# A GpSimd drain between two experts' scatters, and gate logits of the last 256 tokens made token by expert

## The chip, the core and the metric

The kernel runs on one core of a Trainium2 chip. The metric is the device time of one execution in microseconds (us). Three executions are shown for the kernel before, and one execution was profiled.

## What is computed

Three layers one after the other: causal attention with a decay, a dense gated layer, and a mixture of experts that sends each of the 2304 tokens to one of 8 experts. The part that the change touches is the third:

```python
def _moe2_ref(x, w_gate, w_output_gate, w1, w2):
    logits = x @ w_gate                      # (2304, 512) @ (512, 8)
    e_idx = np.argmax(logits, axis=1)
    ...
    gate_w = probs[np.arange(N), e_idx]
    eom = 1.0 / (1.0 + np.exp(-(x @ w_output_gate)))
    for e in range(E):
        mask = e_idx == e
        h = np.maximum(x[mask] @ w1[e], 0.0)
        ye = h @ w2[e]
        out[mask] = gate_w[mask, None] * eom[mask, e, None] * ye
```

## The kernel before

**Attention and the dense layer.** Attention works on 16 pairs of heads. The dense layer (class `MoE1`) runs six groups of 256 hidden columns over chunks of tokens; its result `y` lies in SBUF as feature by token. In the last group the chunks are four of 384 tokens and three of 256 (list `CL`, L912). As soon as a chunk of the last group is done, `Route.chunk` (L434) makes its routing.

**Routing of a chunk.** For each of four blocks of 128 features ScalarE rounds `y` to `yh` (L443), VectorE makes the rest `yl` (L444), and TensorE multiplies with the gate matrix `gw`, 16 columns (8 of the gate, 8 of the output gate) in two parts, as the stationary side and the tokens as the moving side (L445, L446). The product is expert by token. VectorE copies it to SBUF as `lt` (L448), and TensorE transposes it in tiles of 128 tokens to token by expert (L451). `rows` (L505) transposes `y` itself to token rows (L510), and ScalarE copies these out as `yr` (L513), which SyncE writes to the DRAM tensor `yd`. ScalarE copies the second part of the logits as `l0` (L456), VectorE adds the first as `lg` (L457), and then a chain of small VectorE operations follows: maximum (L462), candidates (L464, L465), the expert chosen (L468, L470), ranks of the tokens within their experts with matmuls by `ones` and `U` (L474 to L478), positions (L487 to L495), and for each tile of 128 tokens the matrices `val` and `sel` (L499, L502), whose product (L503) is added into the table `slots`. PSUM tiles of this class come from the pool `rt_ps`, which has two buffers. `finish` (L541) turns `slots` into the lists of token numbers `sl_idx` (L546).

**The experts.** Each expert has 304 slots in tiles of 128, 128 and 48 rows. `MoE2.pull` (L607) gathers its token rows from `yd` by an indirect DMA that GpSimd issues, `gates` (L634) gathers its gate values; both go through `gather` (L639), which keeps the last one in `self.pmark`. `g1` and `g2` are the two matmuls in four quarters. `put` (L685) transposes a tile of the result, scales it by the gates (L696, or L694 on VectorE) and calls `scatter` (L699), an indirect DMA of GpSimd to the rows of `out`. Expert e - 1's three `put` calls come between expert e's quarters (L969 and L970). Tokens beyond an expert's 304 slots go through blocks: one block is worked on between the experts (`block_a` from L973, with gathers of weights through L640, and `block_b` at L979), others in the loop of L985, which runs `trip` times; with these inputs it runs zero times. After the quarters the gates of expert 7 are gathered (L980), the last `g2` runs (L981), and the three last `put` calls follow (L982 and L983).

**What sets the order.** The tile framework traces the calls in this order, orders each engine's instructions and adds semaphores. `tc.issue_after(x)` puts the instructions of its block that run on the engine of `x` behind `x` in that engine's queue, without a wait for its completion. GpSimd's queue holds gathers, scatters, the read of the trip count (L984), the entry of the loop and the end of the program. The engine that is written `POOL` in the profile is GpSimd; a `q` behind an engine's name marks its sequencer.

Of the kernel before, what the change touches and what calls it, by code (L numbers as in the profile page):

```python
# [9 lines left out]
F32 = mybir.dt.float32  # L10
# [10 lines left out]
N = B * S  # L21
# [5 lines left out]
CW = 384  # L27
# [378 lines left out]
class Route:  # L406
# [27 lines left out]
    def chunk(self, t0, n, slots):  # L434
        nc, cst, rp, rp1 = self.nc, self.cst, self.rp, self.rp1
        nt = n // 128
        g0 = t0 // 128
        yc = self.y[:, :, t0:t0 + n]
        lp = self.ps.tile([128, 512], F32, name="rt_ps")
        for k in range(4):  # L440
            yh = rp.tile([128, CW], F32R, name="yh")
            yl = rp.tile([128, CW], F32R, name="yl")
            nc.scalar.activation(yh[:, :n], yc[:, k], ACTF.Copy)  # L443
            nc.vector.tensor_sub(yl[:, :n], yc[:, k], yh[:, :n].bitcast(F32))  # L444
            nc.tensor.matmul(lp[:32, :n], self.gw[:, k], yh[:, :n], start=k == 0, stop=False)  # L445
            nc.tensor.matmul(lp[:16, :n], self.gw[:, k, 0], yl[:, :n], start=False, stop=k == 3)  # L446
        lt = rp1.tile([32, CW], F32, name="lt")
        nc.vector.tensor_copy(lt[:, :n], lp[:32, :n])  # L448
        lp = self.ps.tile([128, 512], F32, name="rt_ps")
        for t in range(nt):  # L450
            nc.tensor.transpose(lp[:, 32 * t:32 * (t + 1)], lt[:, 128 * t:128 * (t + 1)], cst["ident"][:32, :32])  # L451
        self.rows(t0, nt)
        lg = self.lg[:, g0:g0 + nt]
        lv = lp[:, :32 * nt].rearrange("p (t c) -> p t c", t=nt)
        l0 = rp1.tile([128, nt, 16], F32, name="l0")
        nc.scalar.activation(l0, lv[:, :, 16:], ACTF.Copy)  # L456
        nc.vector.tensor_add(lg.rearrange("p t a e -> p t (a e)"), lv[:, :, :16], l0)  # L457
        ll = lg[:, :, 0]
        sm = lambda nm, k=1: rp1.tile([128, nt] if k == 1 else [128, nt, k], F32, name=nm)
        bc = lambda a, k=E_: a.unsqueeze(2).to_broadcast([128, nt, k])  # L460
        mx = self.mx[:, g0:g0 + nt]
        nc.vector.tensor_reduce(out=mx, in_=ll, axis=AX.X, op=ALU.max)  # L462
        cand = sm("cand", E_)
        nc.vector.tensor_tensor(cand, ll, bc(mx), op=ALU.is_ge)  # L464
        nc.vector.scalar_tensor_tensor(cand, cand, -16.0, cst["eiota"].unsqueeze(1).to_broadcast([128, nt, E_]),  # L465
                                       op0=ALU.mult, op1=ALU.add)
        mn = sm("mn_")
        nc.vector.tensor_reduce(out=mn, in_=cand, axis=AX.X, op=ALU.min)  # L468
        oh = self.oh[:, g0:g0 + nt]
        nc.vector.tensor_tensor(oh, cand, bc(mn), op=ALU.is_equal)  # L470
        ohf = oh.bitcast(F32)
        rk = self.ps.tile([128, 512], F32, name="rt_ps")
        rv = rk[:, :nt * E_].rearrange("p (t e) -> p t e", e=E_)
        nc.tensor.matmul(rv, cst["ones"], self.acc.unsqueeze(1).to_broadcast([128, nt, E_]), start=True, stop=False)  # L474
        nc.tensor.matmul(rv, cst["U"], oh, start=False, stop=nt == 1)
        for t in range(nt - 1):
            m = nt - 1 - t
            nc.tensor.matmul(rv[:, t + 1:], cst["ones"], oh[:, t:t + 1].to_broadcast([128, m, E_]),  # L478
                             start=False, stop=m == 1)
        base = sm("base")  # L480
        nc.vector.tensor_scalar(base, mn, 16.0, float(PB * 128), op0=ALU.add, op1=ALU.mult)
        for t in range(nt):
            nc.vector.tensor_add(self.acc, self.acc.bitcast(F32), ohf[:, t])
        pf = sm("pf")
        rs = sm("rs_", E_)
        for t in range(nt):
            nc.vector.tensor_tensor_reduce(out=rs[:, t], in0=rv[:, t], in1=ohf[:, t], scale=1.0, scalar=base[:, t:t + 1],  # L487
                                           op0=ALU.mult, op1=ALU.add, accum_out=pf[:, t:t + 1])
        pi = rp1.tile([128, nt], I32, name="pi")
        nc.vector.tensor_copy(pi, pf)  # L490
        li = rp1.tile([128, 2, nt], I32, name="li")
        nc.vector.tensor_scalar(li[:, 0], pi, 127, 0, op0=ALU.bitwise_and, op1=ALU.logical_shift_right)
        nc.vector.tensor_scalar(li[:, 1], pi, 7, 0, op0=ALU.logical_shift_right, op1=ALU.logical_shift_right)
        lf = rp1.tile([128, 2, nt], F32, name="lf")
        nc.vector.tensor_copy(lf, li)  # L495
        for t in range(nt):
            g = g0 + t
            val = rp.tile([128, NBLK], F32R, name="val_")
            nc.vector.tensor_scalar(val, cst["iota"][:, :NBLK], lf[:, 1, t:t + 1], cst["tok1"][:, g:g + 1],  # L499
                                    op0=ALU.is_equal, op1=ALU.mult)  # L500
            sel = rp.tile([128, 128], F32R, name="sel_")
            nc.vector.tensor_scalar(sel, cst["iota"][:, :128], lf[:, 0, t:t + 1], None, op0=ALU.is_equal)  # L502
            nc.tensor.matmul(slots[:, :NBLK], sel, val, start=(g == 0), stop=(g == NT - 1))  # L503
# [87 lines left out]
class MoE2:  # L591
# [107 lines left out]
    def scatter(self, o, ix, free=True):  # L699
        ins = self.nc.gpsimd.indirect_dma_start(out=self.out, out_offset=bass.IndirectOffsetOnAxis(ap=ix, axis=0),  # L700
                                                in_=o, in_offset=None, bounds_check=N - 1, oob_is_err=False)
        if free:
            if self.nput:
                self.tc.declare_no_dep(ins.ins, group="rows", reason="each token row is scattered by one slot only")
            self.tc.add_to_no_dep_group("rows", ins.ins)
            self.nput += 1
# [161 lines left out]
def tile_kernel(tc, io, out, dbg=None):  # L868
    nc = tc.nc
    with ExitStack() as ctx:  # L870
# [65 lines left out]
        with ExitStack() as c2:  # L936
            wc = pool(c2, "wC", 12, reuse_waits="tile")
            wts.pools = [wab[0], wc, wc]
            m2 = MoE2(tc, c2, cst, io, wts, rt.yd, rt.gd, info, out)
            pblk = pool(c2, "blk")  # L940
            m2.braw = pool(c2, "blk_raw")
            cur = cp.tile([128, 1], F32, name="cur")
            nc.vector.memset(cur, 0.0)
            gwk = pool(c2, "gwk")
            m2.L[0, 0] = w00
            with tc.issue_after(rt.mark[0].ins), tc.issue_after(rt.mark[1].ins):
                m2.pull(0)
                m2.warm(WARM[0], info["id1"])
                for t in range(NSB):
                    m2.pre(0, t)  # L950
                    m2.warm(WARM[1 + t], m2.YG[0][min(t, 1)])
            with tc.issue_after(m2.mark[0].ins), tc.issue_after(m2.mark[1].ins):
                for u in range(1, 4):
                    m2.L[0, u] = load_expert(nc, io, wts, m2.raw, 0, u)
            st = [(e, u) for e in range(E_) for u in range(4)]
            for i, (e, u) in enumerate(st):
                if u == P0 and e + 1 < E_:
                    m2.pull(e + 1)
                if u == 0 and e:
                    m2.gates(e - 1)  # L960
                m2.g1(e, u)
                if i == GI:
                    rt.gate_rows(m2.ps_g, gwk)
                    rt.blocks(info, gwk)
                if u >= P1 and u < P1 + NSB and e + 1 < E_:
                    m2.pre(e + 1, u - P1)
                if i:
                    m2.g2(*st[i - 1])
                if u < NSB and e:  # L969
                    m2.put(e - 1, u)  # L970
                if (e, u) == (4, 3):
                    with tc.issue_after(m2.pmark.ins):
                        blk = m2.block_a(pblk, cur, rt)  # L973
                if e == 5:
                    with tc.issue_after(m2.pmark.ins):
                        blk[4](2)
                if (e, u) == (6, 2):
                    with tc.issue_after(m2.mark[0].ins), tc.issue_after(m2.mark[1].ins):
                        m2.block_b(pblk, cur, True, blk)  # L979
            m2.gates(E_ - 1)  # L980
            m2.g2(*st[-1])  # L981
            for t in range(NSB):  # L982
                m2.put(E_ - 1, t)  # L983
            trip = nc.values_load(info["trip"][0:1, 0:1], min_val=0, max_val=NOB + E_)  # L984
            with tc.For_i(0, trip, 1):  # L985
                m2.block(pblk, cur, rt, False)
# [35 lines left out]
```

## Time and profile before

| What | Time |
|---|---|
| Three runs | 1008.58, 1012.9, 1015.99 us |
| Median | 1012.9 us |
| Profiled execution, own time | 1005.57 us |
| Its span, first to last instruction | 1003.8 us |
| Granted TensorE clock over the span | 0.975 |

The span is what the rows below are taken from; 1.8 us of the profiled execution's time lie around it. The profiled execution was 7.3 us faster than the median of the three runs.

### The profile page before, as it was taken

To read this page: it belongs to the slowest core of one execution; us is meant where nothing else is said; L and a number is where in the kernel's file an instruction comes from. 1 tells how busy PE (TensorE), PEld (TensorE's weight loads), DVE (VectorE), ACT (ScalarE), POOL (GpSimd) and SP (SyncE) were. 2 spreads that over 40 slices of the span, in tenths; PEclk is the share of its full clock that TensorE was granted. 3 is DMA by queue.
4 is the path that set the end of the run, shared out by engine and by line. 5 is a ranking of instruction groups with operands and counts; after the bars stand their busy time and mean duration, and the time that the engine had idled before them with its cause. 6 is when DMAs were issued, how large, how long until landed. Compare 5 with 4: busy or idle time off the path is not lost.

```text
span 1003.8 us, 16493 instructions
## 1 busy us (share of the span) xinstructions
PE 944.4 (94%) x6282; PEld 847.5 (84%) x6282; DVE 597.3 (60%) x1421; ACT 411.9 (41%) x903; POOL 228.4 (23%) x205
## 2 busy tenths in 40 slices
PE   8899999999999999999999999999899999699893
PEld 5555555579999999999999999998799999699692
DVE  6566776759457468468467455677865554343720
ACT  5556666644343132132132123333554555244620
POOL 1244444442021011011011000000244434631111
PEclk9999999999999999999999999999899999989997
DMA  5344444313122012012012000113576576750400
GB/s 165 102 130 114 143 134 136 107 43 105 43 64 63 1 53 74 1 47 81 1 42 64 1 1 22 43 58 133 185 226 185 183 229 184 231 174 27 132 30 25
DMA packets 53088, 94.83 MB, mean 94 GB/s; under 512 B 5954, under 2 KB 27086, under 8 KB 53007
## 3 DMA queue, kind: packets, MB, share of 16 engines
q1 hardware_dynamic: 47503, 79.58, 26.0%
q0 software_dynamic: 5504, 14.17, 4.2%
q8 instruction: 50, 0.82, 0.3%
q14 instruction: 31, 0.25, 0.1%
HBM read 84.10 MB, written 10.16 MB: 94 GB/s over the span
## 4 chain that ended last, share of the span: by engine, by line
PE 57%; issue 16%; DVE 12%; POOL 6%; ACT 3%; DMA 3%; POOLq 0%; SPq 0%; DVEq 0%; ACTq 0%
PE ps_g L365 23%; PE ps_y L383 12%; PE ps_s L144 4%; DVE dt L316 3%; PE avy L201 3%; PE ps_t L185 3%; PE m_psg L659 3%; PE m_psy L674 2%; PE avx L201 2%; POOL out L700 2%; DVE dt L317 1%; ACT e L158 1%; POOL w L329 1%; DVE e L151 1%; DVE dt L315 1%
## 5 line engine op out<-in xcount | busy, mean ns | idle before, releaser
L365 PE MATMUL ps_g<-xth,w 128*128 128x384 f32 (+1 forms) x1184 | 308.6, 331 | 0.0
L365 PEld LDWEIGHTS ps_g<-xth,w 128*128 128x128 f32 x1184 | 213.1, 188 | 0.6
L365 PE MATMUL ps_g<-xtl,w 128*128 128x384 f32 (+1 forms) x592 | 196.1, 331 | 0.0
L383 PE MATMUL ps_y<-hh,w 128*128 128x384 f32 (+1 forms) x592 | 161.2, 333 | 2.9 <-DVE y L389 2.2
L659 PE MATMUL m_psg<-ygh,w 128*128 128x304 f32 x512 | 117.4, 311 | 1.2 <-ACT b_o L809 0.8
L674 PE MATMUL m_psy<-h2h,w 128*128 128x304 f32 x512 | 114.6, 306 | 0.5 <-issue 0.5
L383 PEld LDWEIGHTS ps_y<-hh,w 128*128 128x128 f32 x592 | 107.1, 188 | 5.8 <-DVE y L389 4.0
L329 POOL TENSOR_TENSOR w<-ds,w 128x512 fp32r<-128x512 f32 x36 | 49.8, 1384 | 271.9 <-ACT w L328 271.4
L365 PEld LDWEIGHTS ps_g<-xtl,w 128*128 128x128 f32 x592 | 111.2, 188 | 0.1
L158 ACT ACTIVATE e<-e,mx 128x320 f32<-128x320 f32 (+4 forms) x160 | 88.5, 555 | 51.7 <-DVE mx L151 51.2
L586 DVE TENSOR_TENSOR w<-raw,w 128x1024 fp32r<-128x1024 f32 x64 | 76.8, 1222 | 37.9 <-ACT w L585 22.4
L383 PE MATMUL ps_y<-hl,w 128*128 128x384 f32 (+1 forms) x296 | 97.9, 331 | 0.5 <-DVE hl L373 0.5
L372 ACT ACTIVATE hh<-hs 128x384 fp32r<-128x384 f32 (+1 forms) x74 | 38.2, 517 | 134.4 <-DVE hs L371 134.4
L370 DVE SCALAR_TENSOR_TENSOR hs<-hs,ps_g 128x384 f32<-128x384 f32 (+1 forms) x74 | 40.0, 541 | 86.4 <-ACT hs L369 86.4
L659 PEld LDWEIGHTS m_psg<-ygh,w 128*128 128x128 f32 x512 | 87.4, 193 | 1.8 <-ACT b_o L809 0.9
L674 PEld LDWEIGHTS m_psy<-h2h,w 128*128 128x128 f32 x512 | 85.5, 188 | 0.3
L151 DVE CUSTOM_DVE_ANT_0 e<-ps_s,mask 128x320 f32<-128x320 f32 (+4 forms) x160 | 62.6, 429 | 37.5 <-PE ps_s L144 36.6
L585 ACT ACTIVATE w<-raw 128x1024 fp32r<-128x1024 f32 x64 | 67.5, 1059 | 34.1 <-PE m_psg L659 13.3
L659 PE MATMUL m_psg<-ygl,w 128*128 128x304 f32 x256 | 78.4, 306 | 0.5 <-DVE ygl L627 0.5
L389 DVE TENSOR_TENSOR y<-ps_y,y 128x384 f32<-128x384 f32 (+1 forms) x124 | 67.2, 542 | 19.0 <-PE ps_y L383 18.2
L369 ACT ACTIVATE hs<-ps_g 128x384 f32<-128x384 f32 (+1 forms) x74 | 35.4, 479 | 104.6 <-PE ps_g L365 104.5
L674 PE MATMUL m_psy<-h2l,w 128*128 128x304 f32 x256 | 77.4, 302 | 0.0
(305 smaller groups left out, 1520.0 us busy)
## 6 DMA issues: line engine op xcount, KB each, us to landing
raw<-w SPq DMA_DIRECT2D x64, 512.0 KB
qk<-qk SPq DMA_DIRECT2D x16, 576.0 KB
v<-vL SPq DMA_DIRECT2D x16, 448.0 KB
raw<-mg SPq DMA_DIRECT2D x12, 512.0 KB
raw<-mv SPq DMA_DIRECT2D x12, 512.0 KB
raw<-mo SPq DMA_DIRECT2D x12, 512.0 KB
rb<-rd SPq DMA_DIRECT2D x16, 288.0 KB
yd<-yr SPq DMA_DIRECT2D x18, 256.0 KB
```

The source lines that it names most:

```text
L144: nc.tensor.matmul(ps[a][b:, :n], x, y, start=c == 0, stop=c == 1, tile_position=(h, b))
L151: nc.vector.tensor_tensor_reduce(out=o, in0=x, in1=y, scale=-0.125, scalar=BIGF if prev[a] is None else prev[a][b:], op0=ALU.add, op1=ALU. ...
L158: nc.scalar.activation(es[a][b:, :w], es[a][b:, :w], ACTF.Exp, bias=prev[a][b:], scale=-1.0, accum_out=rs[b:, c:c + 1])
L201: nc.tensor.matmul(self.X[x][64 * a:64 * a + 64, d0:d0 + n], v[k0:k0 + k, a, j], self.T[g, a][k0:k0 + k, o:o + n], start=g == 0, stop=g == ...
L329: nc.gpsimd.tensor_sub(lo, s3, hi.bitcast(F32))
L365: nc.tensor.matmul(ps[:, :n], w[:, k, fs], x[:, k], start=(k == 0 and c == 0), stop=(k == 3 and c == 2))
L383: nc.tensor.matmul(ps[:, :n], w[:, f, ds], h[:, f, :n], start=(f == 0 and c == 0), stop=(f == 1 and c == 2))
L389: nc.vector.tensor_add(y, ps[:, :n], y)
L585: nc.scalar.activation(hi, r, ACTF.Copy)
L586: nc.vector.tensor_sub(lo, r, hi.bitcast(F32))
L659: nc.tensor.matmul(ps[:, :C], w[:, k, fs], x[:, k], start=(k == 0 and c == 0), stop=(k == 3 and c == 2))
L674: nc.tensor.matmul(self.P[e][d][:, :C], w[:, f, ds], h[:, f], start=(u == 0 and f == 0 and c == 0), stop=(u == 3 and f == 1 and c == 2))
```

## The change

Two edits. In `Route.chunk`, for the chunk that ends at the last token (the last 256), the sides of the logit matmuls are exchanged: tiles of 128 tokens of `yh` and `yl` are the stationary side and `gw` the moving one, so that the product is token by expert at once, and the copy `lt` and its transposes are left out. In the main program a drain of GpSimd is issued behind the last gather and the last scatter traced so far, those of `gates(7)` and of expert 6's third tile, and the three scatters of expert 7 come behind it.

```diff
@@ Route.chunk
         g0 = t0 // 128
+        last = t0 + n == N
         yc = self.y[:, :, t0:t0 + n]
...
             nc.vector.tensor_sub(yl[:, :n], yc[:, k], yh[:, :n].bitcast(F32))
+            if last:
+                for t in range(nt):
+                    ts = slice(128 * t, 128 * (t + 1))
+                    nc.tensor.matmul(lp[:, 32 * t:32 * (t + 1)], yh[:, ts], self.gw[:, k], start=k + t == 0, stop=False)
+                    nc.tensor.matmul(lp[:, 32 * t:32 * t + 16], yl[:, ts], self.gw[:, k, 0], start=False,
+                                     stop=k == 3 and t == nt - 1)
+                continue
             nc.tensor.matmul(lp[:32, :n], self.gw[:, k], yh[:, :n], start=k == 0, stop=False)
             nc.tensor.matmul(lp[:16, :n], self.gw[:, k, 0], yl[:, :n], start=False, stop=k == 3)
-        lt = rp1.tile([32, CW], F32, name="lt")
-        nc.vector.tensor_copy(lt[:, :n], lp[:32, :n])
-        lp = self.ps.tile([128, 512], F32, name="rt_ps")
-        for t in range(nt):
-            nc.tensor.transpose(lp[:, 32 * t:32 * (t + 1)], lt[:, 128 * t:128 * (t + 1)], cst["ident"][:32, :32])
+        if not last:
+            lt = rp1.tile([32, CW], F32, name="lt")
+            nc.vector.tensor_copy(lt[:, :n], lp[:32, :n])
+            lp = self.ps.tile([128, 512], F32, name="rt_ps")
+            for t in range(nt):
+                nc.tensor.transpose(lp[:, 32 * t:32 * (t + 1)], lt[:, 128 * t:128 * (t + 1)], cst["ident"][:32, :32])
@@ MoE2.scatter
+        self.smark = ins
@@ tile_kernel
             m2.gates(E_ - 1)
+            with tc.issue_after(m2.pmark.ins), tc.issue_after(m2.smark.ins):
+                dr = nc.gpsimd.drain()
             m2.g2(*st[-1])
-            for t in range(NSB):
-                m2.put(E_ - 1, t)
+            with tc.issue_after(dr.ins):
+                for t in range(NSB):
+                    m2.put(E_ - 1, t)
```

## Rows read from the trace of the kernel before

**Rows 1.** The page, busy time by engine (us, share of the span, instructions)

```profile
PE 944.4 (94%) x6282; PEld 847.5 (84%) x6282; DVE 597.3 (60%) x1421; ACT 411.9 (41%) x903; POOL 228.4 (23%) x205
```

**Rows 2.** Stretches: length, busy PE PEld DVE ACT POOL, PEclk, DMA share, GB/s

```profile
992.00:994.00 2.00, 0.00 (x0) 0.00 (x0) 0.00 (x0) 0.00 (x0) 0.00 (x0) 0.50 0.00 0
...
995.60:1003.00 7.40, 0.00 (x0) 0.00 (x0) 0.00 (x0) 0.00 (x0) 0.00 (x0) 0.50 0.00 1
```

**Rows 3.** Line L1018, program's end: ns min/median/max, first and last start in us

```profile
L1018 POOLq DRAIN  x3: 46/108/7277, 995.7 to 1003.5; - x3
...
L1018 DVEq DRAIN  x2: 10/14/17, 995.3 to 1003.2; - x2
```

**Rows 4.** Line L985, loop entry, GpSimd's sequencer, the same view

```profile
L985 POOLq INC_SWDGE_SEM  x1: 1919/1919/1919, 992.0 to 992.0; - x1
```

**Rows 5.** Line L1015, program's start, GpSimd's sequencer, the same view

```profile
L1015 POOLq INC_SWDGE_SEM  x1: 27/27/27, 0.1 to 0.1; - x1
...
L1015 POOLq DRAIN  x1: 169/169/169, 0.3 to 0.3; - x1
```

**Rows 6.** Timeline, last chunk's logits: start us, us, engine, line, operation

```profile
699.37 0.28 PE L445 MATMUL rt_ps<-yh,gw 128*32 128x256 f32 x1
...
699.48 0.28 PE L446 MATMUL rt_ps<-yl,gw 128*16 128x256 f32 x1
...
700.74 0.29 PE L446 MATMUL rt_ps<-yl,gw 128*16 128x256 f32 x1
...
701.07 0.41 DVE L448 COPY lt<-rt_ps 32x256 f32<-32x256 f32 x1
701.41 0.34 DVE L499 TENSOR_SCALAR val__7402<-cst,lf 128x152 fp32r<-128x152 f32 x1
...
701.54 0.31 PE L451 MATMUL rt_ps<-cst,lt 32*128 32x32 f32 x2 [0.50 <-DVE lt L448]
...
701.77 0.42 PEld L510 LDWEIGHTS rt_ps<-cst,y 128*128 128x128 f32 x4
...
701.88 0.20 ACT L456 ACTIVATE l<-rt_ps 128x32 f32<-128x32 f32 x1 [1.73 <-PE rt_ps L451]
...
702.14 0.27 DVE L502 TENSOR_SCALAR sel__7409<-cst,lf 128x128 fp32r<-128x128 f32 x1
...
702.33 0.17 DVE L457 TENSOR_TENSOR lg_all<-rt_ps,l 128x32 f32<-128x32 f32 x1
...
707.83 1.28 POOL L640 DMA_INDIRECT yg<-yd,sl_idx  x1 [168.35 <-DVE sl_idx L546]
```

**Rows 7.** Line L640, all gathers that GpSimd issues, the view of rows 3

```profile
L640 POOL DMA_INDIRECT yg<-yd,sl_idx x24: 922/1026/1703, 707.8 to 904.3; - x24
L640 POOL DMA_INDIRECT gate<-gd,sl_idx x24: 931/1004/1521, 742.5 to 903.1; - x24
L640 POOL DMA_INDIRECT b_r<-w,b_wi x12: 997/1002/1212, 802.7 to 875.6; - x12
L640 POOL DMA_INDIRECT b_y<-yd,b_d x1: 1446/1446/1446, 833.2 to 833.2; - x1
L640 POOL DMA_INDIRECT b_g<-gd,b_d x1: 1005/1005/1005, 834.9 to 834.9; - x1
```

**Rows 8.** Line L700, all scatters that GpSimd issues, the view of rows 3

```profile
L700 POOL DMA_INDIRECT out<-o,sl_idx x24: 887/1246/1777, 755.0 to 989.4; - x24
L700 POOL DMA_INDIRECT out<-b_o,b_d x1: 1274/1274/1274, 951.5 to 951.5; - x1
```

**Rows 9.** Timeline of GpSimd, 970 to 991 us

```profile
975.94 0.90 POOL L700 DMA_INDIRECT out<-o,sl_idx  x1 [6.17 <-ACT o L696]
986.82 0.99 POOL L700 DMA_INDIRECT out<-o,sl_idx  x1 [9.99 <-ACT o L696]
988.12 0.98 POOL L700 DMA_INDIRECT out<-o,sl_idx  x1 [0.30 <-issue]
989.41 0.89 POOL L700 DMA_INDIRECT out<-o,sl_idx  x1 [0.30 <-issue]
```

## The prediction, made before the changed kernel was run

> **What bounds the kernel now.** I read the page first, then the end of the span by stretches, then the sequencer rows of the last source lines, then the queue of GpSimd, and last the timeline around the final routing chunk. The page says that TensorE is busy for 94% of the span [rows 1], so most edits elsewhere would be hidden under it. The stretches of the end show where that isn't so [rows 2]: from 992 us on no engine has anything busy, and from 995.6 to 1003 us, 7.4 us, even the DMA share is 0.00. The page's chain does not explain this, because it ends at the last scatter. The sequencer rows of the program's end (L1018) do [rows 3]: the DRAIN of VectorE takes 10 to 17 ns, but GpSimd executes three, of 46, 108 and 7277 ns, the long one first, at 995.7 us. 995.7 + 7.28 gives 1003.0, and the span ends at 1003.8: everybody waits for GpSimd's drain. Just ahead of it, in the barrier at the loop of L985, which runs zero times here, GpSimd spends 1919 ns on one INC_SWDGE_SEM at 992.0 [rows 4]. At the start of the program, with no transfer of GpSimd behind them, the same two operations cost 27 and 169 ns [rows 5]. So 9.2 us of the end are two sequencer instructions of GpSimd, with all data already landed.
>
> The second place that the change touches is the hand-over from the dense layer to the experts, at 699 to 708 us, where TensorE waits for a chain of small VectorE operations and GpSimd's first gather waits until 707.83 [rows 6].
>
> **Part one, the drain.** What does the long drain pay for? Since the start GpSimd has issued 24 + 24 + 12 + 1 + 1 gathers (L640) [rows 7] and 24 + 1 scatters (L700) [rows 8], 87 in all. The two drains behind the long one find no new transfer and cost 46 and 108 ns; so the long one clears something that stays cleared. If that is one record for each of GpSimd's transfers, one costs (7277 - 108) / 87 = 82 ns. The change drains after the 84th, so the last drain has three left: 108 + 3 x 82 = 355 ns. It gives back 7277 - 355 = 6.92 us on the bare end of the span. The bounds are 7277 - 46 = 7.23 us and, if the price is for a queue that was used at all, nothing.
>
> The early drain itself: it stands behind the scatter of expert 6's last rows, which starts at 975.94 and takes 0.90, so it begins at 976.84 at the latest. Behind it on GpSimd wait the three scatters of expert 7, the first at 986.82 when ScalarE has made its rows [rows 9], then GpSimd's read of the trip count and the loop's barrier. 84 records take 6.9 us, to 983.7. If it must first wait for the transfers in flight, I add at most 1.7 us (the last scatter's issue ends at 990.30, and the DMA share is gone by 992 [rows 2, 9]): 985.4. That is 1.4 us ahead of need, so I cost the early drain at nothing; its cover is expert 7's matmuls, which don't use GpSimd. Without that cover, each microsecond past 986.82 moves all three scatters, which follow each other without a gap, and so the end, by a microsecond. The bounds of its length are 46 ns and, since one and the same scatter takes from 887 to 1777 ns here [rows 8], twice 7.28, 14.6 us; I take 6.9, the row of the same operation scaled by its count.
>
> INC_SWDGE_SEM: the trace has it at 1919 ns with 87 transfers behind it and at 27 ns with none. Nothing shows how it depends on them; a gain is bounded by 0 and 1.89 us. I take 1.4, three quarters: the operation is the same, as it was for the drain, but at the program's start it may also have fewer semaphores to handle. With a short drain the next thing late is the last scatter's transfers, which I leave as they are.
>
> A rule that speaks against this part: the Trainium skill, "VectorE: DVE Perf Modes", section "The DRAIN you can't avoid", says that drains of the preamble and postamble are boilerplate of about 12 ns on all five engines. VectorE's drains here, 10 to 17 ns, agree; GpSimd's 7277 ns doesn't [rows 3]. By that rule the added drain would cost about 12 ns and clear nothing, the 7.28 us would belong to something else that the last row happens to cover, and the time would be that of the first rival below.
>
> **Part two, the logits of the last 256 tokens.** Removed: VectorE's copy of the logits (L448), which holds that engine from 701.07 until the next operation starts at 701.41, 0.34 us; two transposes on TensorE at 701.54; and the hand-overs around them. Before, the last logit matmul starts at 700.74, ScalarE's copy l0 at 701.88 and the sum lg at 702.33 [rows 6]. Added: 16 matmuls with a stationary side of 128 tokens in place of 8 with 256 moving tokens. A load of 128 x 128 takes 0.42 / 4 = 0.11 us from one to the next (L510), the old pairs 0.11 (699.37 to 699.48) [rows 6], and the two transposes took 0.31, so 16 x 0.11 - 8 x 0.11 - 0.31 = 0.6 us more of TensorE, most of it in its waits for yh and yl. Three of them follow the last yl: 700.74 + 3 x 0.11, plus the 0.34 that lay between the start of the transposes and l0 at 701.88, gives l0 at about 701.4, half a microsecond sooner. But VectorE is not free then: val and sel of the chunk before (701.41 to 702.14) stand ahead of lg, and they move up only by the 0.34 us of the copy. If lg is put ahead of them it gains up to 0.8, and they come back later in the same chain. I take 0.34 us, and bounds of -0.6 (all the added TensorE work bare) and +0.8. The chain behind lg ends in the gather at 707.83, so the 0.34 is passed on to the experts. The chunk takes one buffer of rt_ps less; the row transposes (L510) may start earlier for the first tile and wait for lg for the second, and neither has a follower before the ranks are needed. No DMA is added or moved past another queue.
>
> **Sum.** 6.92 + 1.4 + 0.34 = 8.7 us. The profiled execution took 1005.6 us with a span of 1003.8; it becomes 996.9. It lies 7.3 us under the median of the shown runs, 1012.9; the terms don't depend on what makes the runs differ, so I take the same 8.7 us from the median: 1004.2 us, 0.86% less.
>
> **The rivals.**
> First, the drain's price is fixed, or is not the drain's: every drain after use costs 7.28 us, or the added one costs next to nothing. For it: the trace has no drain after few transfers, so that the price grows with their count is not shown. Against it: the price was gone for the two drains behind the long one, as it would be if it were paid for records that are then cleared. Only part two is left: 1012.9 - 0.3 = 1012.6.
>
> Second, the early drain is slowed beside running work, by as much as scatters are (a factor 2 in [rows 8]): 14.6 us from 976.84 ends at 991.4, 4.6 us past need, while the last one is short all the same. 8.7 - 4.6 = 4.1: 1008.8. Against it: the stretch has a light VectorE and little DMA, and the scatters there take 0.90 to 0.99 [rows 9], the low end.
>
> Third, slower than before: the price is for a used queue and not for a count, and the early drain is slowed as well. The place is the queue of GpSimd ahead of 986.82; it decides as soon as the early drain takes more than 10.0 us (986.82 - 976.84), as nothing is given back at the end. At 14.6 us: +4.6 - 0.3, 1017.2. Against it: it needs both of the above at once.
>
> **How the numbers follow.** Forecast 0.80, first rival 0.13, second 0.05, third 0.02. The forecast's own range is 1003.3 to 1006.6 (INC_SWDGE_SEM from 0 to 1.89, part two from -0.6 to +0.8). The range given: down to the three upper bounds, 7.23 + 1.89 + 0.8 = 9.9, and the lowest shown run (4.3 under the median), 1012.9 - 9.9 - 4.3 = 998.7, rounded to 999; up to the second rival and the highest shown run (3.1 above the median), 1011.9, rounded to 1012. Left out are a good half of the first rival, the third, and the tails, some 0.17. A measurement of this kernel tells about 1%, 10.1 us, from no change. The forecast lies 1.4 us short of that, inside what runs scatter, so I give a third of it to faster: 0.27. Slower by over 1% would need the third rival with an early drain of over 20 us, or a bad draw of the first: 0.02. The rest is 0.71.
>
> **What would show it.** Right: a second long DRAIN of GpSimd, some 7 us, that starts near 977 us; the last first drain under 0.5 us; INC_SWDGE_SEM under 1 us; the first scatter of expert 7 still ready with its rows; the gather of expert 0 at about 707.5. Wrong: a last drain that still takes 7 us, an added drain of nanoseconds, or a scatter of expert 7 that starts right where the added drain ends.

## The result, and the profile after

The changed kernel takes 1000.42 us (median of 8 runs, 995.82 to 1003.49). The kernel before, run beside it, has a median of 1009.16 us over 8 runs, lower than the 1012.9 us of the three that were known. By these medians the gain is 8.74 us, 0.87%. The ratio on record, which is taken over the runs and isn't the quotient of the two medians, is 0.9902, with a 95% interval of 0.9874 to 0.9931: 0.98% faster. The interval lies clear of no change, the gain is just under the 1% that the prediction took as the least that a measurement tells, and by a 2% verdict it is "same". The profiled execution of the changed kernel took 1001.02 us, with a span of 999.2.

Here is the page of the changed kernel, busy time by engine, the line that answers to [rows 1]:

```profile
PE 944.8 (95%) x6288; PEld 848.4 (85%) x6288; DVE 598.5 (60%) x1420; ACT 411.2 (41%) x903; POOL 229.2 (23%) x205
```

Nothing in it tells of the gain. TensorE has 6 matmul instructions more: 16 in place of 8, without the two transposes. VectorE has one instruction less, the copy. No engine works less than before by more than a microsecond, because the time that went was never busy time on this page.

It is found where [rows 3 to 5] were found. These are GpSimd's sequencer rows of the changed kernel by source line (ns min/median/max, first and last start in us); the change moves the lines, so L1031 is the program's end, L998 the loop's entry, L992 the added drain and L1028 the program's start:

```profile
L1031 POOLq DRAIN  x3: 52/98/302, 998.1 to 999.0; - x3
...
L1031 DVEq DRAIN  x2: 10/14/17, 997.7 to 998.7; - x2
...
L998 POOLq INC_SWDGE_SEM  x1: 244/244/244, 996.1 to 996.1; - x1
...
L992 POOLq DRAIN  x1: 8069/8069/8069, 979.2 to 979.2; - x1
...
L1028 POOLq INC_SWDGE_SEM  x1: 27/27/27, 0.1 to 0.1; - x1
...
L1028 POOLq DRAIN  x1: 174/174/174, 0.3 to 0.3; - x1
```

The long drain of the end is gone: 7277 ns became 302. INC_SWDGE_SEM went from 1919 to 244. The long one now stands on L992. It starts at 979.24 us, while the scatter ahead of it is still to be issued, and its 8069 ns contain that wait; it ends at 987.31. GpSimd's own timeline of the changed kernel tells the rest (start us, us, what it is, and in brackets the idle time ahead of it and what ended it):

```profile
979.47 0.90 POOL L709 DMA_INDIRECT out<-o,sl_idx  x1 [6.17 <-ACT o L705]
990.36 0.99 POOL L709 DMA_INDIRECT out<-o,sl_idx  x1 [9.99 <-ACT o L705]
991.66 0.98 POOL L709 DMA_INDIRECT out<-o,sl_idx  x1 [0.30 <-issue]
992.94 0.89 POOL L709 DMA_INDIRECT out<-o,sl_idx  x1 [0.30 <-issue]
```

Expert 6's last scatter ends at 979.47 + 0.90 = 980.37. The drain's own work is what lies behind that, 987.31 - 980.37 = 6.94 us. The first scatter of expert 7 starts 3.05 us later. Its idle time ahead, 9.99 us, is the same to the hundredth as before, and was ended by the same releaser, the rows that ScalarE makes [rows 9]. So the drain is there in full and nobody waits for it.

The end itself in stretches, as in [rows 2] (length, busy time of PE, PEld, DVE, ACT and POOL, granted clock, DMA share, GB/s); the second stretch lies within the first:

```profile
993.90:996.10 2.20, 0.00 (x0) 0.00 (x0) 0.00 (x0) 0.00 (x0) 0.00 (x0) 0.80 0.18 48
995.20:996.10 0.90, 0.00 (x0) 0.00 (x0) 0.00 (x0) 0.00 (x0) 0.00 (x0) 0.51 0.00 0
996.20:999.00 2.80, 0.00 (x0) 0.00 (x0) 0.00 (x0) 0.00 (x0) 0.00 (x0) 0.50 0.02 6
```

Behind INC_SWDGE_SEM, which starts at 996.1, only some 2.8 us are left, and no seven empty microseconds stand in them any more. From the end of the last scatter's issue to the end of the span it was 1003.8 - 990.30 = 13.5 us and is 999.2 - 993.83 = 5.4, so 8.1 us less. The sum over it: drain -6.98, INC_SWDGE_SEM -1.68, and +0.55 given back, as 2.30 us in place of 1.75 pass from the end of the last scatter's issue to INC_SWDGE_SEM. That last stretch is from 1.7 to 2.4 us over all the profiles of this study, 2.4 in the second run below, which has no early drain; so it isn't laid to the change.

The two spans differ by 4.6 us only. The last sum of the dense layer starts at 699.16 us before and at 703.21 after, so the changed kernel's profiled execution was 4.05 us late before either edit had done anything. Expert 0's first gather, which is at 707.83 before [rows 6], is this row after:

```profile
711.92 1.29 POOL L649 DMA_INDIRECT yg<-yd,sl_idx  x1 [168.39 <-DVE sl_idx L555]
```

So from the last sum to that gather it took 8.67 us before and 8.71 after, and from the gather to the end of the last scatter's issue 282.47 and 281.91. With the end: 4.05 + 0.04 - 0.56 - 8.1 = -4.6. The second edit, the logits, has gained nothing: 8.71 for 8.67. (In the other profiles below that keep the new logits as they are, this stretch is 8.61 to 8.98 us, so two or three tenths in it are scatter.)

### The profile page after: what moved, and what is told of

It reads as the page before. It is cut to its first block, busy times and chain, and to the rows that moved or that the text cites. A ratio compares the mean times of both kernels' runs of the same rounds, so it can differ in the third digit from the quotient of the medians.

```text
span 999.2 us, 16507 instructions
## 1 busy us (share of the span) xinstructions
PE 944.8 (95%) x6288; PEld 848.4 (85%) x6288; DVE 598.5 (60%) x1420; ACT 411.2 (41%) x903; POOL 229.2 (23%) x205
## 4 chain that ended last, share of the span: by engine, by line
PE 51%; issue 20%; DVE 12%; POOL 8%; DMA 4%; ACT 4%; POOLq 0%; SPq 0%; DVEq 0%; ACTq 0%
PE ps_g L365 23%; PE ps_y L383 12%; PE ps_s L144 4%; DVE dt L316 3%; PE ps_t L185 3%; PE avy L201 3%; POOL out L709 2%; PE avx L201 2%; POOL gate L649 2%; DVE dt L317 2%; POOL yg L649 2%; DVE dt L315 1%; ACT e L158 1%; POOL w L329 1%; DMA raw<-w 1%
## 5 line engine op out<-in xcount | busy, mean ns | idle before, releaser
L389 DVE TENSOR_TENSOR y<-ps_y,y 128x384 f32<-128x384 f32 (+1 forms) x124 | 67.1, 542 | 19.0 <-PE ps_y L383 18.2
```

What stands on the lines that cost most here:

```text
L389: nc.vector.tensor_add(y, ps[:, :n], y)
```

## Experiments

The first four were run on one chip beside 17 runs of the kernel before (median 1006.38 us), the other three on another chip, again beside 17 (median 993.78 us). Ratios are those on record, to the kernel before on the same chip; the changed kernel as it is wasn't run beside them. The edits are shown against the changed kernel. All profiles are single executions.

**The drain alone.** The logits stay as they were before the change.

```diff
-        last = t0 + n == N
+        last = False
```

> The changed kernel with the drain alone; the logits of the last 256 tokens are made as before. Theory C (each drain of GpSimd pays some 82 ns for every transfer issued since the last drain, and the early one lies under expert 7's matmuls): nearly the whole gain, the end of the span shorter by 8.1 to 8.7 us from the last scatter's issue on, ratio to the kernel before 0.9905 to 0.9925. Rival G (the new logits carry a part of the gain that the two profiles hide): 0.993 or more.

Measured: 998.84 us, ratio 0.9916 [0.9893, 0.9938]. Its GpSimd rows by line, as above:

```profile
L1031 POOLq DRAIN  x3: 52/98/302, 996.9 to 997.7; - x3
...
L998 POOLq INC_SWDGE_SEM  x1: 244/244/244, 994.9 to 994.9; - x1
...
L992 POOLq DRAIN  x1: 8069/8069/8069, 978.4 to 978.4; - x1
```

The same three durations to the nanosecond. From the end of the last scatter's issue to the end of the span it is 5.0 us, 8.5 less than before. The drain alone makes the whole gain that can be measured; its interval holds the ratio of the changed kernel.

**The logits alone.** The drain is left out, and the three scatters of expert 7 stand behind the rest as before.

```diff
-            with tc.issue_after(m2.pmark.ins), tc.issue_after(m2.smark.ins):
-                dr = nc.gpsimd.drain()
             m2.g2(*st[-1])
-            with tc.issue_after(dr.ins):
-                for t in range(NSB):
-                    m2.put(E_ - 1, t)
+            for t in range(NSB):
+                m2.put(E_ - 1, t)
```

> The changed kernel without the drain. Theory C: the last drain is back at 7.2 to 7.4 us and INC_SWDGE_SEM at 1.9 us, and from the last y sum to expert 0's first gather it takes 8.6 to 8.8 us as in both profiles, so ratio 0.998 to 1.002. Rival G (the logits gain the forecast 0.34 us or more): that stretch is 8.3 us or less; at 2 us of gain or more the ratio would be under 0.998.

Measured: 1007.63 us, ratio 1.0015 [0.9996, 1.0035]: no gain. The two long durations of the end are those of the kernel before, to the nanosecond:

```profile
L1028 POOLq DRAIN  x3: 46/108/7277, 997.7 to 1005.6; - x3
...
L995 POOLq INC_SWDGE_SEM  x1: 1919/1919/1919, 994.1 to 994.1; - x1
```

From the last sum of the dense layer to expert 0's first gather it took 8.98 us, above the 8.6 to 8.8 that had been expected, and with the drain alone 8.59. So the logits as changed shorten nothing there.

**Why the logits gain nothing.** The timelines show it. This is the kernel before, in the last chunk (L389 the sum, L443 the copy yh, L444 the difference yl):

```profile
699.16 0.42 DVE L389 TENSOR_TENSOR y<-ps_y,y 128x256 f32<-128x256 f32 x1
699.27 0.88 ACT L443 ACTIVATE yh<-y 128x256 fp32r<-128x256 f32 x2 [0.61 <-PE rt_ps L445]
...
699.86 0.42 DVE L444 TENSOR_TENSOR yl<-y,yh 128x256 fp32r<-128x256 f32 x1
700.27 0.42 DVE L444 TENSOR_TENSOR yl<-y,yh 128x256 fp32r<-128x256 f32 x1
```

And the changed kernel in the same place (the lines are now L444 and L445, and the logit matmuls L449 and L450):

```profile
703.21 0.42 DVE L389 TENSOR_TENSOR y<-ps_y,y 128x256 f32<-128x256 f32 x1
...
703.76 0.86 ACT L444 ACTIVATE yh<-y 128x256 fp32r<-128x256 f32 x2 [1.07 <-PE rt_ps L449]
...
704.21 0.43 DVE L445 TENSOR_TENSOR yl<-y,yh 128x256 fp32r<-128x256 f32 x1 [0.21 <-ACT yh L444]
704.66 0.42 DVE L445 TENSOR_TENSOR yl<-y,yh 128x256 fp32r<-128x256 f32 x1
...
705.48 0.36 DVE L508 TENSOR_SCALAR val__7402<-cst,lf 128x152 fp32r<-128x152 f32 x1
...
706.41 0.18 DVE L466 TENSOR_TENSOR lg_all<-rt_ps,l 128x32 f32<-128x32 f32 x1
```

The third yh starts 0.11 us after the last sum before and 0.55 after; ScalarE's idle time ahead of it grew from 0.61 to 1.07 us, and the matmuls of the logits end it. The pool of yh has two buffers. The third yh takes the one that the first block's matmuls read, and a block now has four matmuls in place of two. So yl comes 0.3 us later on VectorE (0.70 and 1.11 after the last sum before, 1.00 and 1.45 after), and the first operation of the chunk before that follows (val) starts 2.27 us after the last sum, where it started 2.25 before [rows 6], although the copy ahead of it is gone. lg: 3.20 and 3.17; in each of the six profiles with the new logits and shared buffers it is 3.20. To try this, the third and fourth yh of the last chunk get buffers of their own:

```diff
-            yh = rp.tile([128, CW], F32R, name="yh")
+            yh = rp1.tile([128, n], F32R, name=f"yh{k}") if last and k > 1 else rp.tile([128, CW], F32R, name="yh")
```

> The changed kernel, but in the last chunk the third and the fourth yh have buffers of their own, so that they don't wait until TensorE has read the first and second. Theory Y (the exchanged matmuls hold yh longer, and that wait ate the gain of the logits): the third yh starts some 0.4 us earlier against the last y sum, and from that sum to expert 0's first gather it takes 8.2 to 8.4 us in place of 8.7. Rival V (VectorE's order of work in the stretch ate it): the third yh is earlier, but the stretch stays at 8.6 to 8.8 us. Ratio by both within 0.001 of the changed kernel's.

Measured: 1001.0 us, ratio 0.993 [0.9904, 0.9955]. Its timeline in the same place:

```profile
703.63 0.42 ACT L444 ACTIVATE yh<-y 128x256 fp32r<-128x256 f32 x1 [0.26 <-DVE y L389]
703.88 0.42 DVE L389 TENSOR_TENSOR y<-ps_y,y 128x256 f32<-128x256 f32 x1
704.34 0.42 ACT L444 ACTIVATE yh<-y 128x256 fp32r<-128x256 f32 x1 [0.30 <-DVE y L389]
...
705.82 0.36 DVE L508 TENSOR_SCALAR val__7402<-cst,lf 128x152 fp32r<-128x152 f32 x1
...
712.17 1.29 POOL L649 DMA_INDIRECT yg<-yd,sl_idx  x1 [167.97 <-DVE sl_idx L555]
```

Both yh now wait for VectorE's sums of the dense layer (y) and not for matmuls. The third starts 0.25 us ahead of the last sum, 0.8 us earlier than with the shared buffers, where 0.4 had been expected. The two yl are back where the kernel before has them (0.71 and 1.13 us after the last sum), and val starts 1.94 us after it: 0.33 less than in the changed kernel and 0.31 less than before, close to the 0.34 that had been forecast. The gather comes 712.17 - 703.88 = 8.29 us after the sum, 0.42 less than in the changed kernel, but tenths of that are scatter, as said above, so the 0.33 at val is the better figure. The wait for yh's buffer is thus shown to be what ate the gain. The old logits were not run with buffers of their own; their rows above show nothing that such buffers could give, as VectorE begins yl there without a wait for yh, while in the changed kernel it waits 0.21 us. The total can't confirm three tenths of a microsecond: the ratio is 0.0028 above that of the changed kernel, where 0.001 had been expected, but inside its interval and that of the drain alone.

**The drain earlier, with few transfers behind it.** It is moved to expert 4's third quarter, where 54 transfers have been issued; 33 are left for the end.

```diff
                 if u < NSB and e:
                     m2.put(e - 1, u)
+                if (e, u) == (4, 2):
+                    with tc.issue_after(m2.pmark.ins), tc.issue_after(m2.smark.ins):
+                        nc.gpsimd.drain()
...
-            with tc.issue_after(m2.pmark.ins), tc.issue_after(m2.smark.ins):
-                dr = nc.gpsimd.drain()
             m2.g2(*st[-1])
-            with tc.issue_after(dr.ins):
-                for t in range(NSB):
-                    m2.put(E_ - 1, t)
+            for t in range(NSB):
+                m2.put(E_ - 1, t)
```

> The drain moved to behind expert 3's scatters, some 54 transfers after the start; some 33 are left for the end. Theory C: the moved drain takes some 54 x 82 ns = 4.4 us from the end of the scatter's issue ahead of it, the last one 0.1 + 33 x 0.082 = 2.8 us, INC_SWDGE_SEM between 0.5 and 1.2 us; the end is some 3 us longer than in the changed kernel, ratio 0.993 to 0.996. Rival F (the first drain after GpSimd's first transfer pays a price of some 7 us once, whatever its count, and later ones are cheap): the moved one takes 7 us, the last one 0.1 to 0.3 us, ratio 0.989 to 0.992.

Measured: 997.37 us, ratio 0.99 [0.9881, 0.992]. GpSimd's rows by line (L983 is the drain that was moved):

```profile
L1031 POOLq DRAIN  x3: 52/98/2752, 993.6 to 996.9; - x3
...
L998 POOLq INC_SWDGE_SEM  x1: 844/844/844, 991.0 to 991.0; - x1
...
L983 POOLq DRAIN  x1: 7530/7530/7530, 856.9 to 856.9; - x1
```

The last drain takes 2752 ns for 33 transfers and 302 for 3: (2752 - 302) / 30 = 82 ns for one. That is the count's price once more, and a price that is fixed, or not the drain's, falls; so does that of the expectation's rival, paid once by the first drain, since the last one would then have cost 0.1 to 0.3 us. The time from the last scatter's issue to the end of the span is 8.3 us, 3 us more than in the changed kernel, as the count wants. The median of the six runs isn't longer, though, so the expectation on the ratio, 0.993 to 0.996, missed. In the profile the stretch from expert 0's first gather to the end of the last scatter's issue is 278.96 us here, 281.3 to 282.5 in the two runs with one edit each and the kernels before and after, and 284.16 in the run with buffers of its own for yh. The difference shows in TensorE's work (the first number behind the length) around the weight gathers of the extra block; the first line is the run with the drain alone, the second this one:

```profile
850.00:900.00 50.00, 41.39 (x288) 40.19 (x288) 20.19 (x28) 19.94 (x31) 23.04 (x21) 0.90 0.66 213
850.00:900.00 50.00, 45.93 (x304) 44.05 (x303) 21.38 (x30) 19.78 (x33) 26.64 (x24) 0.90 0.66 216
```

TensorE is idle for 4.1 us of these 50 here, and for 8.5 to 9.1 in the five other profiles named so far. The drain stands ahead of ten of the twelve weight gathers; the first of the ten starts 158.3 us after expert 0's first gather here and 156.2 with the drain alone. That may have shortened the wait, or it may be chance; it was left to the last experiment. The moved drain also took 5.60 us beyond the scatter ahead of it, where 54 transfers at 82 ns are 4.4.

**The drain without its cover.** It is put between the first and the second scatter of expert 7, so that two scatters stand behind it with their rows ready.

```diff
-            with tc.issue_after(m2.pmark.ins), tc.issue_after(m2.smark.ins):
-                dr = nc.gpsimd.drain()
             m2.g2(*st[-1])
-            with tc.issue_after(dr.ins):
-                for t in range(NSB):
+            for t in range(NSB):
+                if t == 1:
+                    with tc.issue_after(m2.pmark.ins), tc.issue_after(m2.smark.ins):
+                        dr = nc.gpsimd.drain()
+                    with tc.issue_after(dr.ins):
+                        m2.put(E_ - 1, t)
+                elif t == 2:
+                    with tc.issue_after(dr.ins):
+                        m2.put(E_ - 1, t)
+                else:
                     m2.put(E_ - 1, t)
```

> The drain stands between the first and the second of expert 7's three scatters instead of ahead of them. Theory C (whatever stands behind a drain on GpSimd waits until it has gone through its transfers): the second scatter starts some 85 x 82 ns = 7.0 us after the first one's issue has ended, where it was 0.3 us, so the last scatter is 6.7 us later against the first, the end after it is as short as in the changed kernel, and the ratio to the kernel before is 0.996 to 1.000. Rival H (the queue goes on beside a drain): 0.989 to 0.992, with 0.3 us between the scatters.

Measured: 995.22 us, ratio 0.9996 [0.9977, 1.0015]: the whole gain is gone. GpSimd's timeline:

```profile
979.14 0.99 POOL L709 DMA_INDIRECT out<-o,sl_idx  x1 [9.99 <-ACT o L705]
988.01 0.98 POOL L709 DMA_INDIRECT out<-o,sl_idx  x1 [7.88 <-issue]
989.29 0.90 POOL L709 DMA_INDIRECT out<-o,sl_idx  x1 [0.30 <-issue]
```

its drains by line (L995 is the moved one, L1037 the program's end):

```profile
L995 POOLq DRAIN  x1: 8241/8241/8241, 978.9 to 978.9; - x1
...
L1037 POOLq DRAIN  x3: 52/98/220, 993.9 to 994.7; - x3
```

and a stretch of the same kernel, as in the windows above:

```profile
980.50:987.90 7.40, 0.00 (x0) 0.00 (x0) 0.00 (x0) 0.00 (x0) 0.00 (x0) 0.54 0.11 38
```

Between the first and the second scatter 0.30 us pass in the changed kernel, 7.88 here. The view calls that idle time "issue", because it doesn't count the sequencer's drain as work; the stretch shows that no engine works meanwhile. The drain ends at 987.14 us, 7.0 us after the first scatter's issue, as 85 transfers at 82 ns want, and the second scatter starts 0.9 us behind it. The last drain is short (220 ns for two transfers): the end is 4.7 us where the kernel before has 13.5, so 8.8 us are saved there and 7.6 paid ahead of it. The 1.2 us that should be left over, 0.1%, are too few for the total to show. The gain thus depends on the cover, TensorE's matmuls for expert 7.

**More transfers, hardly more rows.** 24 gathers of 8 rows each are added, one ahead of each gate gather, into a tile that nothing reads.

```diff
         g = self.G[e] = self.hp.tile([128, NSB], F32, name="gate")
+        gx = self.hp.tile([128, NSB], F32, name="gx")
         for t, m in enumerate(SZ):
+            self.gather(gx[:8, t:t + 1], self.gd, self.rt["idx"][:8, 0, e * PB + t:e * PB + t + 1])
```

> The changed kernel with 24 more gathers of 8 rows of 4 bytes each into a tile that nobody reads, one beside each gather of gates; the early drain has 108 transfers behind it in place of 84, and some 9100 rows in place of 8900. Theory C (a price for each transfer): the drain ends 108 x 82.6 ns = 8.9 us after the last issue ahead of it, 6.9 in the changed kernel. Rival R (a price for each row or descriptor): 7.1 us.

Measured: a single execution, 993.87 us, so the time says nothing here and the profile has to. Its drain row by line, and the two scatters around the drain on GpSimd's timeline:

```profile
L994 POOLq DRAIN  x1: 10025/10025/10025, 972.1 to 972.1; - x1
```

```profile
972.29 0.89 POOL L711 DMA_INDIRECT out<-o,sl_idx  x1 [6.17 <-ACT o L707]
983.19 0.99 POOL L711 DMA_INDIRECT out<-o,sl_idx  x1 [10.01 <-ACT o L707]
```

The drain ends 8.90 us after the scatter ahead of it, for 108 transfers; the changed kernel's took 6.94 for 84. (8.90 - 6.94) / 24 = 82 ns: a gather of 8 rows costs the drain as much as the larger transfers. What counts is their number, not their rows. The drain ended 1.1 us ahead of the next scatter, which still waited for its rows alone.

**Two drains.** The drain in expert 4 is added, and that of the change stays.

```diff
+                if (e, u) == (4, 2):
+                    with tc.issue_after(m2.pmark.ins), tc.issue_after(m2.smark.ins):
+                        nc.gpsimd.drain()
```

> The changed kernel with a second drain behind expert 3's scatters: some 54 transfers for the first, 30 for the second, 3 for the last. Theory C: the second takes 30 x 82 ns = 2.5 us from the end of the issue ahead of it, and the end of the span is as in the changed kernel. On the stretch of the experts there are two theories. M (the drain in the middle shortens it by some 2 us, as the profile of the moved drain showed, because the ten gathers of weights behind it come later): ratio 0.985 to 0.989. N (that stretch was short by chance): 0.989 to 0.992.

Measured: 986.54 us, ratio 0.9916 [0.9894, 0.9937]. GpSimd's rows by line (L983 the first drain, L995 the second):

```profile
L1034 POOLq DRAIN  x3: 52/98/297, 982.7 to 983.5; - x3
...
L983 POOLq DRAIN  x1: 7374/7374/7374, 856.6 to 856.6; - x1
...
L995 POOLq DRAIN  x1: 3921/3921/3921, 963.7 to 963.7; - x1
```

The second drain has 30 transfers left and takes 2.79 us beyond the scatter ahead of it, where 84 took 6.94: a drain clears what it has paid for. A middle drain that shortens the experts by 3 us would have to show here as another 0.3% beside the gain of the change, 0.987 to 0.989, and the interval begins at 0.9894. But this run couldn't show it. On this chip TensorE has no idle time around the weight gathers even without a middle drain, as this line of the run with the drain put late shows:

```profile
850.00:900.00 50.00, 50.00 (x366) 49.27 (x366) 24.29 (x33) 23.05 (x38) 31.46 (x27) 1.00 0.74 248
```

The run with more transfers and this one have 50.00 there as well, so there was nothing to shorten. Whether the middle drain shortened the experts on the first chip stays open. The six runs there and the 4.1 us of idle time in place of 8.5 to 9.1 speak for it; no run separates it from chance.

## Why the prediction was right, and where it was not

The forecast was 8.7 us less than the kernel before, 0.86%. The medians beside each other give 1009.16 - 1000.42 = 8.74 us; the ratio on record would make it 9.9. The predicted time, 1004.2 us, is 3.8 over the measured one because the three known runs of the kernel before lay 3.7 us above its median over eight. The measured time lies inside the range, and the change inside "within 1%", the case with most of the chance, by two hundredths of a per cent. That the sum came out so closely is luck in part: two terms missed in opposite directions, and the measured gain itself is known to a microsecond at best (8.74 or 9.9).

- **What the long drain pays for** was right: one price for each transfer, 82 ns, cleared once paid. The kernel before had one point on that line. The runs added the end's drain with 2, 3 and 33 transfers and early drains with 84, 85, 108, 30 and 54; the last two are dear (2.79 us where the count gives 2.5, and 5.60 and 5.45 where it gives 4.4). The forecast's 355 ns for the last drain was 302, since its fixed part is some 56 ns and not the 108 of the drain behind it; the gain at the end was 6.98 us for 6.92.
- **That the early drain is hidden** was right, in length and place. It took 6.94 us for the 6.9 forecast, and nothing was added for transfers in flight. It ended 3.05 us ahead of need, and the forecast's 983.7 for 986.82 is 3.1. What the cover is worth was shown by taking it away.
- **INC_SWDGE_SEM** was mis-sized: 1.68 us for 1.4. "Three quarters" was a guess between ends. The runs give a line for it too: 244 ns with 3 transfers, 844 with 33, 1919 with 87, so 20 ns for each and some 184 fixed (231 with 2, in the run with the drain put late, fits to 7 ns). Its row at the program's start, 27 ns, lies off that line.
- **The logits** failed: 0.34 us forecast, none found. The failing step is "they move up only by the 0.34 us of the copy". It took the copy out of VectorE's row of work and left what stands ahead of it in place. But the step before had counted 0.6 us more of TensorE and put it into its waits for yh and yl, and didn't ask what that does to who waits for TensorE: yh has two buffers, TensorE holds each for longer, and the copy's time was lost again in a later yl (by 0.30 and 0.34 us). With buffers of their own for two yh, the 0.34 is there (0.31 at val against the kernel before).
- **The rivals.** That the price is fixed or not the drain's: refuted by the drains of 302, 2752 and 220 ns at the end. That the early drain is slowed beside running work by a factor 2: refuted by 6.94 us, though the drain in expert 4 was 1.0 to 1.2 us longer than its count, there about a quarter. Slower than before, both at once: not seen; the drain put too late, which pays the same 7.6 us by its place, came only to an equal time.
- **The rule weighed.** By the Trainium skill, "VectorE: DVE Perf Modes", section "The DRAIN you can't avoid", drains of the preamble and postamble cost about 12 ns on all five engines. VectorE's again agree (10 to 17 ns), but GpSimd's don't: 302 ns with 3 transfers behind it, 7277 with 87. The measurement decides. Its figure is given for the drains of the preamble and postamble; that it would hold for a drain which a kernel adds was the prediction's reading.

## What to carry to other kernels

Look past the last busy instruction: if the end of a span is empty, read the sequencer rows of the program's last lines, where GpSimd may be paying for each transfer that it has issued, here 82 ns. That work can be done earlier, under matmuls, by a drain behind the last transfer that is known to have a gap behind it; whatever is queued on GpSimd behind the drain waits for it, so the gap must be longer than the count times the price. In expert 4 a drain took up to 1.2 us more than that, and a scatter that had to wait for a drain started 0.9 us behind its end. And when matmuls are exchanged for more and smaller ones, ask how long each operand's buffer is now held, not only how long the engine is busy.

## What was not expected of the hardware

- The price of a drain goes by transfers and not by rows: 82 ns each, for a gather of 8 rows as for a larger one.
- INC_SWDGE_SEM at the loop's entry has the same habit at a lower price, 20 ns for each transfer since the last drain.
- The drain in expert 4 took 5.60 and 5.45 us for 54 transfers, in two profiles, where the count gives 4.4. What the extra microsecond is wasn't tried.
- Around the weight gathers of the extra block TensorE is idle for 8.5 to 9.1 us of the 50 from 850 to 900 us in five profiles (the kernels before and after, and the first three experiments), for 4.1 with the drain in the middle, and for none in the three profiles on the other chip. No edit changes the weight gathers themselves. The cause wasn't tried, and the difference is as large as the gain of the change.
